# Attention and a mixer on one core: sums of weight quarters on GpSimd over two elements, all queries and keys of the first element loaded ahead, its x transposed within the attention

## The chip, the core and the metric

One core of one Trainium2 chip runs the kernel. Its engines work side by side, each with a queue of instructions of its own that it takes in order: TensorE (PE; the profile shows its weight loads apart, as PEld), VectorE (DVE), ScalarE (ACT), GpSimd (POOL), and SyncE (SP), which issues most DMAs. An instruction that waits for a semaphore holds up all that stand behind it on its engine. The metric is the device time of one execution in microseconds (us).

## The reference

Attention with normalised queries and keys, over 8 batch elements, 12 heads, 448 positions and 64 features a head; its result, laid out as 448 x 768 per element, goes through a mixer: a token layer (448 to 256 to 448, over positions) and a channel layer (768 to 1536 to 768), each added to its input.

```python
q_n, k_n = rmsnorm(q, g_q), rmsnorm(k, g_k)          # over the 64 features of a head
attn = softmax(scale * q_n @ k_n.T) @ v
x = attn.transpose(0, 2, 1, 3).reshape(B, S, H * D)
h = relu(x.transpose(0, 2, 1) @ w_tok1) @ w_tok2
u = x + h.transpose(0, 2, 1)
out = u + relu(u @ w_ch1) @ w_ch2
```

q, k and v are 32-bit floats; the four weight matrices arrive as 64-bit floats and are turned into 32-bit ones by the kernel.

## The kernel before, in words

**The queues are written out by hand.** Work is made as lists of items, each a cost and a function that issues instructions. `merge` (L27) takes lists and deals them into one order, so that each list advances by the same share of its own total cost; an item of cost 0 goes with the one before it. The engines get their instructions in just this order. The main loop (L899 to L925) first merges the attention of element 0 with the first weight conversions. Then for each element b it merges the attention of element b + 1 (`att_items`) with the mixer of element b (`middle_items`, `last_items`), so attention runs one element ahead.

**Attention** goes by pairs of heads, six pairs to an element, 48 in all. `load_qk` (L992) loads a pair's queries and keys with six DMAs on SyncE. `squares` (L1012) squares them on ACT and sums each row on DVE, `roots` (L1038) makes the reciprocal roots on DVE by a chain of ten small instructions, `swap` moves two columns, and `scale` (L285) multiplies the queries by their roots. The keys' roots go into the exponential instead. `trans_qk` (L297) transposes queries and keys on TensorE, and ACT copies them out of PSUM, times the gain. `score` and `score_last` multiply and ACT takes exponentials (L315); `av` and `av_last` multiply by v (L426, L438); the row sums of the exponentials are made on TensorE (L405), after GpSimd (L386) and DVE (L392, L397) have added chunks up (from element 1 on); `denominator` divides on DVE. `att_step(g)` (L484) makes the items of step g; four steps serve two pairs. In steps 0 and 1 of four it prepares the two pairs that follow, and in odd steps it loads a pair. The scales stand on GpSimd, except that of pair 0. Pairs 0 and 1 lie in `hb`, which the mixer needs later for its hidden layer, the others in three tiles that they take in turn. At the start, pair 1 is prepared by `second_pair`, after step 0's items, among which are the squares of pair 2.

Scores, transposes of queries and keys, the row sums `d_ps`, and transposes of x share one PSUM pool of four buffers (tag S); the mixer's products share another of two (tag M).

**The weights.** A chunk of 128 x 512 is loaded (`weight_load`), converted in three steps that are spread over three items, on DVE (L215 to L218), ACT (L226, L228), DVE (L235) and GpSimd (L250), and stored as four quarters to DRAM (`store`): 36 such stages, after four chunks of the token weights. Element 0 uses these quarters plainly (`ch1_first`, `ch2_first`). From element 1 on, the channel layer is done with seven products instead of eight (`ch1`, L726, and `ch2`, L783), for which four sums of quarters are needed besides the quarters themselves. `sum_items` (L180) makes them: item i loads the four quarters of stage i from DRAM, makes a difference of stage i - 1 on DVE (L193), two sums of stage i - 2 in one instruction on GpSimd (L196) and a difference of stage i - 3 on DVE (L200), and stores the four of stage i - 4. That is 40 items: 8 are merged with the second channel layer of element 0, 32 with the first layers of element 1. `load_units` (L642) brings the weights for the products from DRAM, up to five units ahead; where the sums that a unit's group needs are not yet recorded as stored, it loads that unit only when its product is issued.

**The mixer.** `trans_x` transposes x (L575; copies by DVE and ACT in turn, L579 and L581), `tok1` (L596) and `tok2` (L604, added on DVE in L609) are the token layer. In `ch1` the seven results are combined on ACT, DVE and GpSimd (L731 to L765); the fifth product's result is added into r on GpSimd, and DVE needs that r to empty the sixth product's PSUM.

## Time and profile before

| | |
|---|---|
| time, median of 3 runs (lowest to highest) | 1483.64 us (1483.38 to 1483.79) |
| the profiled execution, its span | 1483.56 us, 1481.7 us |
| mean granted clock of TensorE | 0.984 |
| busy in the span: ACT, SyncE's DMAs on q1 | 466.8 us (32%), 48.8% of 16 engines |
| DMA traffic | 219.46 MB, mean 148 GB/s |
| landing of a load of quarters, its store | 3.5 us, 3.6 us (median) |

The profile is one execution on the core. A group of instructions is shown by source line, engine, operation, and tiles as output<-input, with busy time and the mean of one, and with the idle time of its engine just ahead of it and what ended that. Matmuls are pipelined, so a busy TensorE is not one at its peak; the granted clock says at which share of full speed it ran. Rows in order of time give the start, the duration, and in brackets the idle time before and its releaser. The releaser is inferred: where the engine named had long been done, it was something else that the instruction waited for.

### The profile page before, as it was taken

What the parts mean: (1) busy time and instruction counts of PE and PEld (TensorE: products, weight loads), DVE (VectorE), ACT (ScalarE), POOL (GpSimd) and SP (SyncE); (2) the same over time, 40 slices, a digit from 0 to 9 for tenths busy, and PEclk for the clock granted to TensorE, in tenths of its full rate; (3) what the DMA queues carried; (4) which work ended last, traced back from release to release, by engine and by line L of the source; (5) the groups of instructions that cost most, each with busy time, mean ns of one, the idle gap of its engine ahead of it and who ended that gap; (6) DMA issues with size and microseconds to landing.
All of it is one profiled execution on the core that took longest, in us unless ns stands there. A gap on an engine that the chain in (4) does not pass through costs nothing.

```text
span 1481.7 us, 19089 instructions
## 1 busy us (share of the span) xinstructions
PE 1404.9 (95%) x6832; PEld 995.9 (67%) x6832; DVE 711.5 (48%) x1332; ACT 466.8 (32%) x798; POOL 402.1 (27%) x370
## 2 busy tenths in 40 slices
PE   4887889999889999999999999999999999999998
PEld 1333334455568867786777857777677947778997
DVE  5787868616565255533544345432544334331321
ACT  4654444222322234323342233322333223312111
POOL 2222323304453123321333123320332212310320
PEclk9898999999999999999999999999999999999999
DMA  5556766736886524554354625454354624434454
GB/s 138 144 164 194 215 187 189 203 90 193 237 250 183 175 74 139 135 162 113 105 155 127 180 56 156 130 152 129 104 147 126 179 60 129 126 120 133 130 172 122
DMA packets 256810, 219.46 MB, mean 148 GB/s; under 512 B 108004, under 2 KB 215524, under 8 KB 256708
## 3 DMA queue, kind: packets, MB, share of 16 engines
q1 hardware_dynamic: 233506, 206.96, 48.8%
q10 hardware_dynamic: 23074, 11.21, 2.9%
q8 instruction: 56, 0.92, 0.3%
q14 instruction: 46, 0.38, 0.1%
q0 software_dynamic: 128, 0.00, 0.0%
HBM read 188.22 MB, written 29.88 MB: 147 GB/s over the span
## 4 chain that ended last, share of the span: by engine, by line
PE 82%; DVE 8%; DMA 5%; issue 1%; SPq 1%; ACT 1%; POOL 1%; ACTq 0%; DVEq 0%; POOLq 0%
PE m_ps L783 23%; PE m_ps L726 21%; PE s_ps L325 7%; PE o_ps L426 7%; PE m_ps L596 5%; PE m_ps L707 4%; PE m_ps L604 4%; PE t_ps L575 3%; PE m_ps L689 3%; PE t_ps L305 2%; DMA ws<-raw 2%; DMA raw<-ws 2%; PE d_ps L405 2%; PE s_ps L339 1%; PE o_ps L438 1%
## 5 line engine op out<-in xcount | busy, mean ns | idle before, releaser
L783 PE MATMUL m_ps<-hb,unit 128*128 128x224 f32 x1764 | 349.5, 354 | 0.0
L783 PEld LDWEIGHTS m_ps<-hb,unit 128*128 128x128 f32 x1764 | 327.8, 190 | 16.2 <-issue 12.7
L315 ACT ACTIVATE e<-s_ps,rs 128x448 f32<-128x448 f32 x336 | 186.8, 632 | 208.6 <-PE s_ps L325 143.0
L726 PE MATMUL m_ps<-tu,unit 128*128 128x224 f32 x1008 | 204.8, 354 | 2.1 <-DVE hb L731 1.8
L726 PEld LDWEIGHTS m_ps<-tu,unit 128*128 128x128 f32 x1008 | 187.6, 190 | 12.2 <-PE o_ps L426 4.2
L726 PE MATMUL m_ps<-uT,unit 128*128 128x224 f32 x756 | 156.9, 361 | 7.2 <-DVE r L731 3.5
L726 PEld LDWEIGHTS m_ps<-uT,unit 128*128 128x128 f32 x756 | 142.7, 192 | 26.3 <-issue 16.4
L325 PE MATMUL s_ps<-qkT 64*128 64x448 f32 x576 | 141.1, 589 | 2.2 <-ACT qkT L307 1.8
L426 PE MATMUL o_ps<-e,v 128*64 128x448 f32 x576 | 133.3, 566 | 0.0
L295 POOL TENSOR_TENSOR qk<-qk,rs 112x512 f32<-112x512 f32 x46 | 51.5, 1141 | 293.8 <-DVE rs L1063 181.0
L792 POOL TENSOR_TENSOR uT<-uT,r 128x448 f32<-128x448 f32 (+1 forms) x56 | 51.1, 922 | 229.3 <-DVE r L792 147.9
L386 POOL TENSOR_TENSOR es<-e 128x896 f32<-128x896 f32 x42 | 89.7, 2136 | 67.2 <-ACT sq L1025 52.7
L596 PE MATMUL m_ps<-x,w_sb 112*128 112x384 f32 x256 | 92.5, 507 | 8.9 <-DVE x L581 8.9
L307 ACT ACTIVATE qkT<-t_ps,g_t 128x448 f32<-128x448 f32 (+1 forms) x96 | 60.8, 658 | 122.4 <-PE t_ps L305 120.6
L325 PEld LDWEIGHTS s_ps<-qkT 64*128 64x128 f32 x576 | 50.7, 191 | 69.2 <-issue 56.6
L467 DVE STREAM_TRANSPOSE dt<-d_ps 128x448 f32<-128x448 f32 x42 | 27.2, 649 | 142.3 <-PE d_ps L405 142.3
L426 PEld LDWEIGHTS o_ps<-e,v 128*64 128x64 f32 x576 | 33.2, 138 | 86.9 <-issue 83.1
L732 ACT ACTIVATE hb<-hb 128x448 f32<-128x448 f32 x63 | 36.5, 579 | 173.6 <-DVE hb L731 148.2
L792 DVE TENSOR_TENSOR uT<-uT,m_ps 128x448 f32<-128x448 f32 (+1 forms) x70 | 34.0, 502 | 116.5 <-PE m_ps L783 116.4
L392 DVE TENSOR_TENSOR es<-es,e 128x896 f32<-128x896 f32 x42 | 46.6, 1110 | 81.9 <-ACT e L315 64.4
L1029 DVE TENSOR_REDUCE ms<-sq 128x16 f32<-128x1040 f32 (+2 forms) x49 | 59.2, 1207 | 52.5 <-ACT sq L1025 49.4
L731 DVE TENSOR_TENSOR r<-m_ps,r 128x448 f32<-128x448 f32 x63 | 39.2, 621 | 94.2 <-POOL r L731 54.5
(94 smaller groups left out, 1607.6 us busy)
## 6 DMA issues: line engine op xcount, KB each, us to landing
unit<-ws SPq DMA_DIRECT2D x318, 384.0 KB, 3.3
raw<-in_moe_w_ch_dram SPq DMA_DIRECT2D x72, 256.0 KB, 3.4
out_dram<-y ACTq DMA_DIRECT2D x48, 224.0 KB, 3.3
qk<-in_q_dram SPq DMA_DIRECT2D x92, 112.0 KB, 3.5
v<-in_v_dram SPq DMA_DIRECT2D x48, 192.0 KB, 2.7
ws<-stage SPq DMA_DIRECT2D x36, 256.0 KB, 3.7
raw<-ws SPq DMA_DIRECT2D x36, 256.0 KB, 3.5
ws<-raw SPq DMA_DIRECT2D x36, 256.0 KB, 3.6
```

Of the source, the lines that this page charges most:

```text
L307: nc.scalar.mul(to, ps[:, 0:NS * n], g_t[:, i:i + 1])
L315: nc.scalar.activation(out=out, in_=ps[:, 0:S], func=AF.Exp, scale=st["rs", p][:, r:r + 1])
L325: nc.tensor.matmul(out=pss[a][:, 0:S], lhsT=qkT[a * D:(a + 1) * D, o:o + P], rhs=qkT[a * D:(a + 1) * D, 0:S], start=True, stop=True)
L386: nc.gpsimd.tensor_tensor(out=es[:], in0=st["e", p, 0][:], in1=st["e", p, 1][:], op=ALU.add)
L426: nc.tensor.matmul(out=o[a * D:(a + 1) * D, 0:S], lhsT=vt[:, c:c + D], rhs=e[:, a, :], start=start, stop=stop)
L596: nc.tensor.matmul(out=ps[:, 0:HC], lhsT=w1_sb[0:R, c, jc * P:(jc + 1) * P], rhs=st["x", h][0:R, c, :], start=(c == 0), stop=(c == NS - 1))
L604: nc.tensor.matmul(out=ps[:, 0:S], lhsT=st["h1", jc][:, cc * P:(cc + 1) * P], rhs=w2_sb[:, jc].rearrange("p c r -> p (c r)"), start=(jc == ...
L707: nc.tensor.matmul(out=ps[:, 0:S], lhsT=w, rhs=natural(half)[:, :, t, :], start=(half == 0 and t == 0), stop=(half == 1 and t == KF - 1))
L726: nc.tensor.matmul(out=ps[:, j * HS:(j + 1) * HS], lhsT=w[:, t, j, :], rhs=m, start=(t == 0), stop=(t == KC - 1))
L783: nc.tensor.matmul(out=ps[:, j * HS:(j + 1) * HS], lhsT=st["w"](j, t), rhs=hb[:, HB[what], t, :], start=(t == 0), stop=(t == KF - 1))
L792: add = lambda e, o, x, y: e.tensor_tensor(out=o, in0=x, in1=y, op=ALU.add)
L1029: nc.vector.tensor_reduce(out=ms[:, lo:hi], in_=self.sq[0:rows, lo:hi], axis=AX_X, op=ALU.add)
```

## The change

- The sums: all three arithmetic instructions of a stage go to GpSimd, together, two items after the stage's load; the store follows one item later. That makes 39 items, dealt out anew: 6 with the second channel layer of element 0, 6 with the end of element 0, 21 with the first layers of element 1, 6 with its second layer.
- The six pairs of element 0 get places in `hb` and are loaded at the start, between the first five weight chunks. Pair 1 is prepared before the first step; pairs 2 and 3 after step 0, pairs 4 and 5 after step 3, each lot at once. These items now have costs.
- The scales of pairs 1 to 11 go to DVE.
- The first half of x of element 0 (three transposes and their copies) is merged with attention steps 8 to 12, ahead of the token layer; then come the second half's transposes, and the token products after them.
- The squares of queries take only the rows that hold data, so each pair's square is two instructions on ACT, and most of the memsets at the start are replaced by a few.

```diff
@@ -183,27 +183,22 @@
         def one(i):
             n = len(stages)
             if i < n:
-                t = raw_tile()
-                q = st["sum", i] = t[:].rearrange("p n w -> p (n w)").bitcast(F32).rearrange(
-                    "p (q n) -> p q n", q=NQ)
-                st["sum tile", i] = t
-                nc.sync.dma_start(out=q[:, 0:4], in_=slots(i, 0, 4))
-            if 0 <= i - 1 < n:
-                q = st["sum", i - 1]
-                nc.vector.tensor_tensor(out=q[:, 6], in0=q[:, 1], in1=q[:, 0], op=ALU.subtract)
+                t = st["sum", i] = raw_tile()
+                nc.sync.dma_start(out=eight(t)[:, 0:4], in_=slots(i, 0, 4))
             if 0 <= i - 2 < n:
-                q = st["sum", i - 2]
+                q = eight(st["sum", i - 2])
+                nc.gpsimd.tensor_tensor(out=q[:, 6], in0=q[:, 1], in1=q[:, 0], op=ALU.subtract)
                 nc.gpsimd.tensor_tensor(
                     out=q[:, 4:6], in0=q[:, 1:7:5], in1=q[:, 3:4].to_broadcast([P, 2, P]), op=ALU.add)
+                nc.gpsimd.tensor_tensor(out=q[:, 7], in0=q[:, 2], in1=q[:, 5], op=ALU.subtract)
             if 0 <= i - 3 < n:
-                q = st["sum", i - 3]
-                nc.vector.tensor_tensor(out=q[:, 7], in0=q[:, 2], in1=q[:, 5], op=ALU.subtract)
-            if 0 <= i - 4 < n:
-                nc.sync.dma_start(out=slots(i - 4, 4, 8), in_=st.pop(("sum", i - 4))[:, 4:8])
-                st.pop(("sum tile", i - 4))
-                st["summed"] = i - 4 if i - 4 < n - 1 else n
+                nc.sync.dma_start(out=slots(i - 3, 4, 8), in_=eight(st.pop(("sum", i - 3)))[:, 4:8])
+                st["summed"] = i - 3 if i - 3 < n - 1 else n
                 load_units(st["at"])
-        return [(1.0, lambda i=i: one(i)) for i in range(len(stages) + 4)]
+
+        def eight(t):
+            return t[:].rearrange("p n w -> p (n w)").bitcast(F32).rearrange("p (q n) -> p q n", q=NQ)
+        return [(1.0, lambda i=i: one(i)) for i in range(len(stages) + 3)]
 
     def convert_first(i):
 
@@ -553,16 +548,23 @@
             items += [(0.5, lambda pp=pp, part=part: chunk_sums(pp, part)) for pp, part in parts]
         if live and s % 2 == 1 and p + (s + 1) // 2 < NP:
             items.append((0.0, lambda: load_v(p + (s + 1) // 2)))
-        if live and s < 2 and p + 2 + s < NP:
-            items.append((0.0, lambda: pre.squares(p + 2 + s, st)))
-            if s == 1:
-                items.append((0.0, lambda: pre.roots(p + 2, 2, st)))
-                items.append((0.0, lambda: swap(p + 3)))
-                items += [(0.0, lambda i=i: scale(p + 2 + i)) for i in range(2)]
+
+        n = p + 2
+        if g in (0, 3):
+            n = 2 if g == 0 else 4
+            items += [(0.3, lambda i=i: pre.squares(n + i, st)) for i in range(2)]
+        elif live and s < 2 and NPAIR <= n < NP:
+            items.append((0.0, lambda: pre.squares(n + s, st)))
+        if g in (0, 3) or live and s == 1 and NPAIR <= n < NP:
+
+            items.append((0.3 * (n < NPAIR), lambda: pre.roots(n, 2, st)))
+            items.append((0.0, lambda: swap(n + 1)))
+            eng = nc.vector if n < 2 * NPAIR else nc.gpsimd
+            items += [(0.3 * (n < NPAIR), lambda i=i: scale(n + i, eng)) for i in range(2)]
         if turned:
             if not inside:
                 items += [(0.4, lambda i=i: trans_qk(q, i)) for i in range(2)]
-            if q + 3 < NP:
+            if NPAIR <= q + 3 < NP:
                 items.append((0.0, lambda: pre.load_qk(q + 3, st)))
         return items
 
@@ -844,12 +846,13 @@
         items += [(us(6, HS), lambda mp=mp, i=i: ch1(b, mp, i)) for mp in range(KF // 2) for i in range(7)]
         return items, [(us(6, HS), lambda i=i, j=j: ch2(b, 0, i, j)) for i in range(7) for j in range(2)]
 
-    def last_items(b):
+    def last_items(b, sums):
 
 
         single = [(us(6, HS), lambda i=i: ch2(b, 1, i, 0)) for i in range(7)]
         if b == 0:
-            single = [(us(6, S), lambda o=o, h=h: ch2_first(o, h, 2)) for o in range(2) for h in range(2)]
+            single = merge(
+                [(us(6, S), lambda o=o, h=h: ch2_first(o, h, 2)) for o in range(2) for h in range(2)], sums)
         l = turns(b, [0, 1, KC, KC + 1])
         if b + 1 < B:
             l += x_items(b + 1, 0) + x_items(b + 1, 1)
@@ -883,41 +886,38 @@
         trans_qk(0, 0)
     st.pop(("ms", 0))
     load_v(0)
-    weight_load(0)
-    weight_load(1)
-    pre.load_qk(2, st)
-    for i in range(2, 5):
+    for i in range(5):
         weight_load(i)
-    pre.load_qk(3, st)
-
-    def second_pair():
-        pre.squares(1, st)
-        pre.roots(1, 1, st)
-        swap(1)
-        scale(1)
-
+        if 2 + i < NPAIR:
+            pre.load_qk(2 + i, st)
+
+    pre.squares(1, st)
+    pre.roots(1, 1, st)
+    swap(1)
+    scale(1, nc.vector)
     per = NPAIR * 2
     att_items = lambda lo, hi: [it for g in range(lo, hi) for it in att_step(g)]
+
     for _, fn in merge(
-            att_items(0, 1) + [(0.0, second_pair)] + att_items(1, AHEAD * per + 1), weight_items(0, BEFORE)):
+            att_items(0, 8) + merge(att_items(8, AHEAD * per + 1), x_items(0, 0)), weight_items(0, BEFORE)):
         fn()
     left, sums = [], sum_items()
     for b in range(B):
         early, double = middle_items(b)
         if b == 0:
-            begin = [it for h in range(2) for it in x_items(0, h) + tok1_items(0, h)]
+            begin = x_items(0, 1) + tok1_items(0, 0) + tok1_items(0, 1)
             early = merge(begin + early, weight_items(BEFORE, then)) + merge(
-                double, weight_items(then, len(chunks) + 3) + sums[:8])
+                double, weight_items(then, len(chunks) + 3) + sums[:6])
         else:
 
             for _, fn in merge(tok1_items(b, 0), left):
                 fn()
             if b == 1:
-                early = merge(early, sums[8:])
+                early, double = merge(early, sums[12:33]), merge(double, sums[33:])
             early = tok1_items(b, 1) + early + double
         lo = (b + AHEAD) * per + 1
         att = att_items(lo, lo + per) if b + AHEAD < B else []
-        for _, fn in merge(att, early) + last_items(b):
+        for _, fn in merge(att, early) + last_items(b, sums[6:12]):
             fn()
         left = turns(b, [2, KC + 2])
     for _, fn in left:
@@ -941,22 +941,21 @@
 
         n = 2 * self.NS * 2 * D
         flat = self.hb[:].rearrange("p q f s -> p (q f s)")
-        assert flat.shape[-1] >= 2 * n
+        assert flat.shape[-1] >= self.NPAIR * n
         self.st = {}
-        self.qk_t = [const.tile([P, n], F32, name=f"qk_{i}") for i in range(3)]
-        for p in range(2):
-            self.st["qk", p] = flat[:, p * n:(p + 1) * n]
+        qk_t = const.tile([P, 3, n], F32, name="qk_t")
+        self.qk_t = [qk_t[:, i, :] for i in range(3)]
+        hb_t = flat[:, 0:self.NPAIR * n].rearrange("p (i n) -> p i n", n=n)
+        for p in range(self.NPAIR):
+            self.st["qk", p] = hb_t[:, p, :]
         self.v_t = [const.tile([P, (2 * self.NS - 1) * D], F32, name=f"v_{i}") for i in range(2)]
 
         warm = const.tile([P, 1], F32, name="warm")
         nc.vector.memset(warm[:], 1.0)
         nc.scalar.activation(out=warm[:], in_=warm[:], func=AF.Square)
-        self.zeros(nc.vector, self.st["qk", 0])
+        self.zeros(nc.vector, hb_t[:, 0:1])
         self.load_qk(0, self.st, other=nc.scalar)
-        for i, qk in enumerate([self.st["qk", 1]] + self.qk_t):
-            eng = nc.gpsimd if i else nc.vector
-            self.zeros(eng, qk)
-            eng.memset(qk[96:P, 0:n // 2], 0.0)
+        self.zeros(nc.vector, hb_t[:, 1:])
         self.load_qk(1, self.st)
         self.g_t = const.tile([P, 2], F32, name="g_t")
         for i, g in enumerate((g_q, g_k)):
@@ -970,8 +969,11 @@
         self.expo_c = const.tile([P, 1], F32, name="expo_c")
         nc.gpsimd.memset(self.expo_c[:], -896.0 * 2**23)
         self.sq = const.tile([P, 4 * self.NS, D + 1], F32, name="sq")
+
+        nc.gpsimd.memset(self.sq[96:P, 0:2 * self.NS, 0:D], 1.0)
         nc.gpsimd.memset(self.sq[:, 0:4 * self.NS - 2, D:D + 1], D * 1e-6)
         nc.gpsimd.memset(self.sq[:, 4 * self.NS - 2:4 * self.NS, D:D + 1], D * 0.5e-6)
+        self.zeros(nc.gpsimd, qk_t)
         self.st["rs", 0] = const.tile([P, 4 * self.NS], F32, name="rs_0")
         with tc.tile_pool(name="st_0", bufs=1) as self.st_pool:
             self.nt_pool = self.st_pool
@@ -982,8 +984,8 @@
 
         D, P = self.D, 128
         o = qk.shape[-1] - 2 * D
-        eng.memset(qk[D:P, o:o + D], 0.0)
-        eng.memset(qk[0:D, o + D:o + 2 * D], 0.0)
+        eng.memset(qk[D:P, :, o:o + D], 0.0)
+        eng.memset(qk[0:D, :, o + D:o + 2 * D], 0.0)
 
     def heads(self, p):
         b, j = divmod(p, self.NPAIR)
@@ -1022,9 +1024,11 @@
         for lo, hi in halves:
             rows = self.R if hi == 1 else 128
             lo, hi = lo * n, hi * n
-            nc.scalar.activation(
-                out=self.sq[0:rows, lo:hi, 0:D],
-                in_=qk[0:rows, lo * D:hi * D].rearrange("p (r d) -> p r d", d=D), func=AF.Square)
+            for r, at, to in ((self.R, lo, min(hi, n)), (128, max(lo, n), hi)):
+                if at < to:
+                    nc.scalar.activation(
+                        out=self.sq[0:r, at:to, 0:D],
+                        in_=qk[0:r, at * D:to * D].rearrange("p (r d) -> p r d", d=D), func=AF.Square)
             ms = st["ms", p][0:rows, p % 2]
             nc.vector.tensor_reduce(
                 out=ms[:, lo:hi], in_=self.sq[0:rows, lo:hi], axis=AX_X, op=ALU.add)
```

## The prediction

> **What bounds the kernel now.** I read the page first, then the busy time by stage, then the waits of TensorE, then the instructions in order of time around the longest waits. The head of the page:
>
> ```profile
> span 1481.7 us, 19089 instructions
> ...
> PE 1404.9 (95%) x6832; PEld 995.9 (67%) x6832; DVE 711.5 (48%) x1332; ACT 466.8 (32%) x798; POOL 402.1 (27%) x370
> ```
>
> The span is 1481.7 us, the same execution took 1483.56 us, so 1.9 us lie outside; it is within 0.1 us of the median of 1483.64, and I work against 1483.6. TensorE idles only 77 us, so the question is where those are. The busy time by stage (start and end; then busy time and count of PE, weight load, DVE, ACT, POOL; granted clock; DMA share; GB/s), cut at the points where TensorE's order of work changes:
>
> ```profile
> core 0: us, PE busy (x) PEld busy (x) DVE busy (x) ACT busy (x) POOL busy (x), PEclk, DMA share, GB/s
> 0.00:27.30 27.30, 7.06 (x20) 3.34 (x20) 14.70 (x55) 10.58 (x16) 6.57 (x24) 1.00 0.72 177
> 27.30:105.90 78.60, 67.87 (x332) 26.47 (x332) 60.67 (x113) 48.63 (x82) 20.08 (x17) 0.89 0.50 136
> 105.90:222.40 116.50, 96.23 (x326) 43.60 (x324) 89.68 (x138) 49.92 (x86) 33.77 (x26) 0.91 0.68 199
> 222.40:340.00 117.60, 117.40 (x420) 58.59 (x419) 66.66 (x101) 38.51 (x66) 28.30 (x22) 1.00 0.54 153
> 340.00:448.00 108.00, 92.76 (x447) 64.36 (x446) 69.89 (x153) 31.62 (x55) 52.75 (x54) 0.97 0.83 242
> 448.00:1481.70 1033.70, 1023.59 (x5295) 799.58 (x5293) 409.89 (x775) 287.51 (x496) 260.64 (x227) 1.00 0.46 132
> ```
>
> Busy time times clock is the work at full clock. Attention of element 0 (27.3 to 105.9) has 60.4 us of it in 78.6, so 18 are lost; the first layers of element 0 (to 222.4) have 87.6 in 116.5, 29 lost; element 1's first layers (340 to 448) have 90.0 in 108, 18 lost; and 20 go before 27.3. From 222 to 340 and after 448 TensorE is full. So only the early stages and the start of element 1 can pay, some 85 us together, and the change touches just these. There DVE comes next: 77% busy in both early stages. What TensorE waited for, over the span (first two rows of its waits) and then from 340 to 448:
>
> ```profile
> PE t_ps L305 <- POOL hb L295: 10.1, 1, 10.1
> PE t_ps L305 <- POOL stage L250: 9.2, 2, 6.3
> ```
>
> ```profile
> PE m_ps L726 <- DVE hb L731: 4.5, 2, 2.8
> PE m_ps L726 <- DVE r L731: 3.7, 3, 3.0
> PE d_ps L405 <- DVE es L397: 2.9, 2, 2.5
> PE m_ps L604 <- DVE uT L609: 2.5, 2, 1.6
> PE d_ps L405 <- ACT e L315: 1.5, 1, 1.5
> ```
>
> Early it is the preparation of queries and keys; in element 1 nearly every wait names DVE.
>
> **The change, part by part.** *1. The start.* In order of time, with a scale on DVE (first row) for its price:
>
> ```profile
> 9.76 0.69 DVE L295 TENSOR_TENSOR hb<-hb,rs 112x512 f32<-112x512 f32 x1
> ...
> 12.23 4.97 PE L325 MATMUL s_ps<-qkT 64*128 64x448 f32 x12 [0.72 <-ACT qkT L307]
> ...
> 13.08 0.17 DVE L1063 SCALAR_TENSOR_TENSOR rs<-nt,rs 128x8 f32<-128x8 f32 x1
> ...
> 14.24 1.26 SPq L1010 DMA_DIRECT2D qk<-in_k_dram  x2
> ...
> 19.02 1.06 ACT L1025 ACTIVATE sq<-qk 128x1024 f32<-128x1024 f32 x1 [2.24 <-DMA qk<-in_k_dram]
> ...
> 21.38 1.06 ACT L1025 ACTIVATE sq<-hb 128x1024 f32<-128x1024 f32 x1 [1.30 <-DVE ms L1029]
> ...
> 23.50 1.13 ACT L315 ACTIVATE e<-s_ps,rs 128x448 f32<-128x448 f32 x2
> ...
> 26.22 1.04 POOL L295 TENSOR_TENSOR hb<-hb,rs 112x512 f32<-112x512 f32 x1 [19.65 <-DVE rs L1063]
> ...
> 27.32 1.86 PE L305 MATMUL t_ps<-ident,hb 112*128 112x112 f32 x8 [10.12 <-POOL hb L295]
> ...
> 33.61 0.98 PE L339 MATMUL s_ps<-qkT 64*64 64x448 f32 x8
> ...
> 40.26 1.23 ACT L307 ACTIVATE qkT<-t_ps,g_t 128x448 f32<-128x448 f32 x2
> ```
>
> Pair 1's preparation stands behind pair 2's squares, which wait for a load that lands at 19. Its own way from the end of the squares (22.44) to the scale (26.22) is 3.8. Ahead of pair 2, with DVE done with pair 0 at 13.3, pair 1 is scaled on DVE by about 18 (an estimate: 13.3 + 3.8 + 0.69). TensorE's transposes come 9 us sooner. But they do not decide when the next scores start: those need the copies out of PSUM, and ACT's queue now has the squares of pairs 2 and 3 ahead of them. SyncE issues pair 2 until 15.5, then a weight chunk's two DMAs and pair 3's six at 0.63 each, to 20.5; with the same 3.5 from issue to use, pair 3 arrives at 24. Behind it ACT has its squares (1.06, a little more now that they are halved), two passes of a weight chunk (1.4, by the row of L226 in part 2), two exponentials (1.13) and two copies (1.23): 29, against the scores' 33.61 now. That is 4 to 4.5 sooner, less 1.5 to 2 for a TensorE restarting from idle, the price that part 3 finds for such restarts. "At once" is thus an order of issue: pair 5's six, two pairs and two chunks later, are out only near 31. I take -2.5; if the four extra loads slow pair 3, +3; if the squares land early, -6. The memsets that leave GpSimd hide behind the first loads: nothing.
>
> *2. Attention of element 0.* The longest later wait:
>
> ```profile
> 59.71 2.49 POOL L295 TENSOR_TENSOR qk<-qk,rs 112x512 f32<-112x512 f32 x2 [4.68 <-DVE rs L1063]
> ...
> 61.33 2.15 DVE L215 TENSOR_SCALAR e_t<-raw 128x512 uint32<-128x512 uint32 x1
> ...
> 64.83 0.72 ACT L226 ACTIVATE e_t<-e_t,expo_c 128x512 uint32<-128x512 uint32 x1 [5.43 <-DVE e_t L218]
> ...
> 65.37 0.43 DVE L215 TENSOR_SCALAR e_t<-raw 128x512 uint32<-128x512 uint32 x1
> ...
> 66.74 1.83 PE L305 MATMUL t_ps<-ident,qk 112*128 112x112 f32 x8 [6.28 <-POOL stage L250]
> ```
>
> DVE is late with a weight chunk, ACT stands 5.43 before that chunk's pass with the exponentials queued behind it, and TensorE gets no PSUM for its transposes. The change moves eleven scales (pairs 1 to 11) to DVE, 11 x 0.69 = 7.6 us. But the same conversion takes 2.15 beside GpSimd's two scales and 0.43 alone: a pair of scales costs DVE 1.38 there, and gives 1.72 back. I set this to zero; uncovered it is +1.38 for two pairs. The Trainium skill, "SBUF — State Buffer", section "Who interferes with whom", gives this as an exclusive lock on a port that DVE and GpSimd share, the later one blocking fully, also for a DVE instruction with two inputs in SBUF; the trace agrees with 2.15 against 0.43. What remains is order: pairs 4 and 5 are prepared a step or two earlier, in one lump after step 3 (counted from 0), and their loads are long in. The lump (two reductions, roots, scales) still holds DVE for some 8 us, and can hold ACT as above, elsewhere. I take half the 6.28: -3, between -10 (both waits of the 9.2 with their slow restarts) and +4 (the lump stalls step 4 as well). The three transposes of x that come here fill idle TensorE time; each keeps one of four PSUM buffers until its copy, inside the +4.
>
> *3. The first layer's input.* Token mixing waits for copies of the transposed x:
>
> ```profile
> 115.64 7.87 PE L596 MATMUL m_ps<-x,w_sb 112*128 112x384 f32 x16 [5.26 <-DVE x L581]
> ...
> 129.81 4.45 PE L596 MATMUL m_ps<-x,w_sb 112*128 112x384 f32 x8 [3.59 <-DVE x L581]
> ...
> 136.96 2.85 PE L596 MATMUL m_ps<-x,w_sb 112*128 112x384 f32 x8
> ```
>
> Eight at full pace take 2.85; the two runs lost 5.26 + (7.87 - 5.70) = 7.4 and 3.59 + 1.6 = 5.2. The first half of x is now done during attention, so the 7.4 goes. The second half's copies get two products (5.7) as cover, but DVE takes them between conversions, and its conversions are not shortened. I take -7.5, between -12.6 and 0.
>
> *4. The sums.* In element 1, DVE's only wait, its two groups and GpSimd's one, and one moment:
>
> ```profile
> DVE raw L193 <- DMA raw<-ws: 36.1, 18, 4.5
> ```
>
> ```profile
> L193 DVE TENSOR_TENSOR raw<-raw 128x128 f32<-128x128 f32 x29 | 15.2, 523 | 36.3 <-DMA raw<-ws 36.1
> L200 DVE TENSOR_TENSOR raw<-raw 128x128 f32<-128x128 f32 x31 | 12.5, 404 | 0.0
> ```
>
> ```profile
> L196 POOL TENSOR_TENSOR raw<-raw 128x256 f32<-128x256 f32 x30 | 23.4, 785 | 29.4 <-DVE raw L193 25.1 <-PE m_ps L726 3.4 <-POOL es L386 0.3
> ```
>
> ```profile
> 439.29 0.29 DVE L193 TENSOR_TENSOR raw<-raw 128x128 f32<-128x128 f32 x1 [4.31 <-DMA raw<-ws]
> ```
>
> DVE is busy 69.89 and waits 36.1 of 108: it paces the stage, since the subtraction comes one item after its load and the products' adds queue behind it. Afterwards DVE loses the wait and 27.7 of work, and keeps 42. Of the sums 21 fall here, not 31; 12 go where TensorE had no gap. GpSimd takes over: no row shows it at 128x128, so it lies between 0.29 (DVE alone) and 0.785 (GpSimd's twice as wide one); I take 0.45, just above half the latter, since that is the same engine. A stage is then 0.45 + 0.785 + 0.45 = 1.7, and GpSimd has 52.75 - 23.4 + 21 x 1.7 = 65 in a stage of some 97 us, 67%. It computes two items after the load, 9 us at that pitch, beyond the load's wait of 4.5. So of the 18 lost I take 11 back; bounds -16 and 0.
>
> *5. The seam.* The second layer's weights need 30 stages summed; the sums laid into the first layers end at 29, so two units load on demand where the second layer begins. SyncE gets to them only behind a store that waits for GpSimd. No such wait is in the trace; between 0 and the 4.5 of the longest load wait, I take +1.5. The first unit loads of element 1, now fed by sums done before 340, cost nothing. Splitting the squares gives ACT, 32% busy, one instruction more per pair: nothing; on the path it would cost less than an exponential's 0.57 each.
>
> The sum: -2.5 - 3 - 7.5 - 11 + 1.5 = -22.5, so 1461.
>
> **The rivals.** *A. DVE keeps the early pace*: parts 1 to 3 move waits about without removing them. For: the conversions and roots are all still there, and ACT's 5.43 was of this kind. Against: DVE idles 23% of both stages. Only the sums pay: 1483.6 - 11 + 1.5 = 1474.
>
> *B. GpSimd takes DVE's place in element 1*: the adds of L731 and the es sums queue behind 1.7 us blocks, and part 4 yields nothing: 1483.6 - 13 + 1.5 = 1472. For: its share rises from 49% to 67%. Against: its present idle time is a wait for DVE (25.1).
>
> *C. Slower.* In the first layer of element 1, GpSimd's add into r must be done before DVE can empty a PSUM buffer, of which there are two. If each of the 21 blocks falls on that path, the stage loses 21 x 1.7 = 36 instead of 18: +18, and with -13 and +1.5 that is +6.5: 1490. It decides when GpSimd's share comes near the whole, some 95 of 97 us instead of 65, that is, when an op of 128x128 costs 1.2. The Trainium skill, "GPSIMD Engine Reference", section 4.1, speaks for this side: elementwise work belongs on VectorE, about twice as fast. By it the narrow ops would be 0.58 against DVE's 0.29, a stage 1.95 and GpSimd's share 72%; no row here shows one on GpSimd.
>
> *D. All waits named go*, each part at its far end: -6 - 10 - 12.6 - 16 = -45: 1439.
>
> **How the numbers follow.** The forecast, 1461 with its own range of 1450 to 1470, has 0.54; A 0.17, B 0.13, C 0.09, D 0.07. A change of 0.2%, 3 us, is about what a measurement can tell. The forecast, D and most of A and B are faster: 0.86; 0.05 of A and B ends within 0.2%; C is slower: 0.09. The range 1446 to 1478 takes in forecast, A and B, and leaves out C, that 0.05 and about half of D.
>
> **What would show it.** Right: the transposes of pair 1 begin near 18 and step 2's scores near 29; no 5 us wait before the first token mixing; DVE with no wait for raw in element 1, TensorE idle there 3 to 6 us and GpSimd 60 to 70% busy, its 128x128 ops at 0.4 to 0.5 us; a wait of 0 to 4 us for a unit at the second layer. Wrong: TensorE waiting on POOL L731 or es in element 1 for over 10 us (B, C), or ACT waits on DVE of the same total before 222 (A).

## The result, and the profile after

The changed kernel takes 1450.17 us (median of 4 runs, 1447.74 to 1453.44), the kernel before 1483.72 beside it (1483.38 to 1484.2): a ratio of 0.9775, 95% interval 0.9756 to 0.9795, or 33.5 us less. The profiled execution took 1450.25 us with a span of 1448.5, at a mean granted clock of 0.989 (0.984 before). First the head of the page after, then its busy time by stage, with the same columns as in the prediction and cut at the same events: the scores of step 2, the first token product of element 0, and so on to the second channel layer of element 1.

```profile
span 1448.5 us, 19051 instructions
...
PE 1398.2 (97%) x6832; PEld 992.3 (69%) x6832; DVE 681.5 (47%) x1270; ACT 471.5 (33%) x845; POOL 423.3 (29%) x425
```

```profile
core 0: us, PE busy (x) PEld busy (x) DVE busy (x) ACT busy (x) POOL busy (x), PEclk, DMA share, GB/s
0.00:23.90 23.90, 10.59 (x46) 5.20 (x46) 15.86 (x58) 11.38 (x20) 4.18 (x17) 1.00 0.63 158
23.90:107.40 83.50, 71.93 (x345) 28.15 (x345) 64.67 (x126) 50.03 (x90) 15.32 (x13) 0.92 0.58 166
107.40:200.00 92.60, 78.48 (x252) 35.16 (x251) 80.49 (x129) 42.03 (x74) 25.89 (x20) 0.91 0.70 206
200.00:308.60 108.60, 108.60 (x388) 52.31 (x387) 59.12 (x90) 38.62 (x68) 41.38 (x47) 1.00 0.71 207
308.60:413.20 104.60, 103.59 (x506) 70.58 (x505) 51.45 (x92) 37.06 (x67) 65.48 (x85) 1.00 0.69 196
413.20:1448.50 1035.30, 1024.97 (x5304) 800.92 (x5304) 409.89 (x779) 292.39 (x527) 271.04 (x245) 1.00 0.46 135
```

TensorE's idle time fell from 77 to 50 us. In the row from 308.60 to 413.20, which holds element 1 up to its second channel layer, it is busy for 103.59 of 104.60, at full clock. The early rows still show idle time and a clock of 0.91 to 0.92. When the same product starts in the profiled executions of both kernels says where the time went (us from the start of the span; the last column is the whole new set of sums alone in the kernel before, run e1 below):

| TensorE starts | before | after | difference | e1 |
|---|---|---|---|---|
| scores of step 2 | 33.61 | 23.86 | -9.75 | 33.9 |
| first token product, element 0 | 115.64 | 107.37 | -8.3 | 114.0 |
| second token layer, element 0 | 139.65 | 121.65 | -18.0 | 137.65 |
| first channel layer, element 0 | 154.64 | 145.47 | -9.2 | 151.35 |
| second channel layer, element 0 | 248.42 | 235.96 | -12.5 | 243.89 |
| first token product, element 1 | 321.73 | 308.59 | -13.1 | 315.9 |
| second channel layer, element 1 | 447.53 | 413.23 | -34.3 | 420.39 |
| first token product, element 2 | 512.15 | 478.75 | -33.4 | 485.94 |

13.1 us are won before element 1, 20.3 in it, and nothing after it (from element 2's first product to the end both take 970). Single executions differ: the kernels of e2, e4 and e9 below do the early work in the same order as the kernel before and reach element 1 1.4 to 2.8 us sooner, so differences of that size in the table say nothing.

**Element 1.** TensorE's waits between 308.6 and 413.2 (total, times, longest), all there are, and GpSimd's three costliest groups there:

```profile
PE m_ps L728 <- DVE uT L611: 0.8, 1, 0.8
```

```profile
L191 POOL TENSOR_TENSOR raw<-raw 128x256 f32<-128x256 f32 x20 | 15.5, 777 | 1.6
L190 POOL TENSOR_TENSOR raw<-raw 128x128 f32<-128x128 f32 x21 | 12.1, 577 | 0.0
L193 POOL TENSOR_TENSOR raw<-raw 128x128 f32<-128x128 f32 x20 | 10.6, 532 | 1.6
```

The waits of 4.5, 3.7, 2.9 and 2.5 us that named DVE are gone. GpSimd is 63% busy (65.48 of 104.6), and its instructions of 128x128 take 0.53 to 0.58 us.

**The start and the early stages.** In order of time, the first steps:

```profile
18.00 1.02 PE L300 MATMUL t_ps<-ident,hb 112*128 112x112 f32 x8 [1.43 <-ACT sq L1029]
...
21.49 0.63 ACT L1029 ACTIVATE sq<-hb 128x512 f32<-128x512 f32 x1 [0.26 <-DMA hb<-in_k_dram]
...
23.86 0.97 PE L334 MATMUL s_ps<-qkT 64*64 64x448 f32 x4 [1.68 <-ACT e L310]
25.48 1.31 PE L334 MATMUL s_ps<-qkT 64*64 64x448 f32 x4 [0.65 <-ACT qkT L302]
```

Pair 1's transposes begin at 18.00, as forecast, and pair 3's keys have landed by 21.49, where the forecast had 24. The products at 23.86 are pair 0's; those of pair 1, which need its copies out of PSUM, start at 25.48. TensorE's waits over the whole span, the first four:

```profile
PE m_ps L606 <- DVE uT L611: 8.5, 3, 4.6
PE s_ps L334 <- ACT qkT L302: 7.0, 3, 5.7
PE t_ps L300 <- DMA hb<-in_k_dram: 6.2, 1, 6.2
PE s_ps L334 <- ACT e L310: 3.8, 2, 2.1
```

The waits for POOL L295 (10.1) and POOL L250 (9.2) are gone. The 6.2 is the first load of all. New at the top, with 8.5 after 5.5 before, is the second token layer (L606), which waits for its PSUM until DVE has added (L611). In order of time, that wait:

```profile
121.65 3.27 PE L606 MATMUL m_ps<-w_sb,h 128*128 128x448 f32 x8
121.72 1.29 DVE L290 TENSOR_TENSOR qk_t<-qk_t,rs 112x512 f32<-112x512 f32 x2
...
128.87 0.61 DVE L611 TENSOR_TENSOR uT<-uT,m_ps 128x448 f32<-128x448 f32 x1
129.53 3.35 PE L606 MATMUL m_ps<-w_sb,h 128*128 128x448 f32 x4 [4.61 <-DVE uT L611]
```

TensorE reaches the second token layer 18 us earlier, gets two PSUM buffers filled, and then DVE goes through two scales and two conversions before it comes to the add at 128.87. Of the 18 us, 8.8 are given back between there and the first channel layer. The attention of element 0 gives back too: step 2 starts 9.75 sooner, but what follows its last product only 4.3 (101.68 instead of 105.95), with three transposes of x now ahead of it and new waits, such as this one for a PSUM buffer that a transpose of x holds until its copy:

```profile
94.26 1.86 PE L320 MATMUL s_ps<-qkT 64*128 64x448 f32 x2 [2.07 <-DVE x L583]
```

### The profile page after: what moved, and what is told of

Same layout as the page of the kernel before. It is cut to its first block, busy times and chain, and to the rows that moved or that the text cites. A ratio compares the mean times of both kernels' runs of the same rounds, so it can differ in the third digit from the quotient of the medians.

```text
span 1448.5 us, 19051 instructions
## 1 busy us (share of the span) xinstructions
PE 1398.2 (97%) x6832; PEld 992.3 (69%) x6832; DVE 681.5 (47%) x1270; ACT 471.5 (33%) x845; POOL 423.3 (29%) x425
## 4 chain that ended last, share of the span: by engine, by line
PE 88%; DVE 6%; issue 2%; SPq 1%; DMA 1%; ACT 1%; POOL 0%; ACTq 0%; DVEq 0%; POOLq 0%
PE m_ps L728 24%; PE m_ps L785 23%; PE s_ps L320 8%; PE o_ps L421 8%; PE m_ps L598 5%; PE m_ps L606 4%; PE m_ps L709 4%; PE m_ps L691 3%; PE t_ps L577 3%; PE t_ps L300 2%; PE d_ps L400 2%; PE o_ps L433 1%; PE s_ps L334 1%; DVE raw L211 1%; DVE raw L230 1%
## 5 line engine op out<-in xcount | busy, mean ns | idle before, releaser
L728 PE MATMUL m_ps<-uT,unit 128*128 128x224 f32 x756 | 153.8, 356 | 1.8 <-DVE uT L611 1.8
L290 POOL TENSOR_TENSOR qk_t<-qk_t,rs 112x512 f32<-112x512 f32 x36 | 39.3, 1113 | 239.9 <-DVE rs L1067 200.6
L606 PE MATMUL m_ps<-w_sb,h 128*128 128x448 f32 x192 | 80.8, 564 | 8.6 <-DVE uT L611 8.5
L598 PE MATMUL m_ps<-x,w_sb 112*128 112x384 f32 x256 | 88.1, 489 | 0.0
L245 POOL TENSOR_TENSOR stage<-raw 128x512 f32<-128x512 f32 x36 | 41.5, 1154 | 143.5 <-DVE raw L230 66.4
```

What stands on the lines that cost most here:

```text
L598: nc.tensor.matmul(out=ps[:, 0:HC], lhsT=w1_sb[0:R, c, jc * P:(jc + 1) * P], rhs=st["x", h][0:R, c, :], start=(c == 0), stop=(c == NS - 1))
L606: nc.tensor.matmul(out=ps[:, 0:S], lhsT=st["h1", jc][:, cc * P:(cc + 1) * P], rhs=w2_sb[:, jc].rearrange("p c r -> p (c r)"), start=(jc == ...
L728: nc.tensor.matmul(out=ps[:, j * HS:(j + 1) * HS], lhsT=w[:, t, j, :], rhs=m, start=(t == 0), stop=(t == KC - 1))
```

## The experiments

The theory to test was that of the prediction, with a size that was wrong: the sums bring more than forecast because DVE no longer stands behind a load. Its rivals: that it is the dealing of the sums over more stages, the number of buffers, or the engine. For the early part: which of the edits pays, and whether the second token layer's wait can be avoided. Ratios are to runs of the kernel before on the same chip, with 95% intervals.

### e1: all of the new sums, nothing else

The kernel before with the changed `sum_items` and its changed dealing (all lines of the diff that touch `one`, `sums`, `last_items`).

> The kernel before with only the new sums (engines, distance from the load, dealing). In the changed kernel element 1 takes 20 us less from its first token product to element 2's, and the early stages 13 us less. If the sums alone make the former: 1463 to 1465, with TensorE idle for 1 to 3 us in element 1's first layers. Rival: the early stages' gain also eases element 1, and the sums alone give about the 9.5 us of the forecast: 1474.

Measured: 1457.81 us, ratio 0.9833 [0.9816, 0.9849], that is 25 us less, against 9.5 in the sum of the prediction's parts 4 and 5, and below the 1463 to 1465 expected: part of the gain comes before element 1. Element 1, from its first token product to element 2's, takes 170.0 us (190.4 before, 170.2 in the full change). TensorE's waits between 300 and 520:

```profile
PE m_ps L721 <- DVE uT L604: 0.8, 1, 0.8
```

So three quarters of the gain is the sums, and the early parts add only 7.6 in medians.

### e2, e3: the two halves of it

e2 takes the new `one(i)` (three instructions on GpSimd two items after the load, the store at i - 3) and deals as before, 8 items and then the other 31. e3 takes the new dealing only:

```diff
-                double, weight_items(then, len(chunks) + 3) + sums[:8])
+                double, weight_items(then, len(chunks) + 3) + sums[:6])
...
-                early = merge(early, sums[8:])
+                early, double = merge(early, sums[12:33]), merge(double, sums[33:])
...
-        for _, fn in merge(att, early) + last_items(b):
+        for _, fn in merge(att, early) + last_items(b, sums[6:12]):
```

> The kernel before with the sums' arithmetic on GpSimd two items after the load, dealt as before (8 items with element 0's second layer, 31 with element 1's first layers). If DVE's wait for loads was what paced element 1, most of the 20 us goes without the spreading: 1465 to 1469. If GpSimd, at 31 x 1.9 us in that stage, takes DVE's place: 1475 to 1484. If it is the spreading that pays: 1480 or more.

> The kernel before with the sums dealt as in the change (6, 6, 21, the rest) but on the old engines and at the old distances. If DVE's wait for loads paces, 21 of 31 waits stay in the first layers, longer pitch makes each a little shorter, and the rest moves to the second layer: a gain of 6 to 10, 1474 to 1478. If the number of sums and their DMA traffic in that stage was the bound: a gain of 15 or more, 1468 or less.

Measured: e2 1473.78, ratio 0.9933 [0.9916, 0.9949], 9.0 less; e3 1467.5, ratio 0.989 [0.9873, 0.9906], 15.3 less. The two add up to 24.3 of e1's 25, and the dealing, which the prediction had no price for, is the larger. e2 fell between its two expectations; e3 came out where the rival had put it, by which the number of sums in that stage, or their DMA traffic, is the bound. In e3 DVE still makes its differences and still waits for loads (first fence: a row of DVE's waits over the span), and the wait for a unit at the second channel layer that the prediction had expected at the seam appears (second fence: TensorE's waits):

```profile
DVE raw L193 <- DMA raw<-ws: 22.2, 8, 6.7
```

```profile
PE m_ps L783 <- DMA unit<-ws: 2.5, 5, 1.0
```

Between the two channel layers of element 1 (348.0 to 425.8) TensorE no longer idles in e3, with the sums still on DVE:

```profile
348.00:425.80 77.80, 77.78 (x404) 58.65 (x404) 48.24 (x96) 27.43 (x47) 34.67 (x36) 0.98 0.77 216
```

In e2 GpSimd has all 31 items in the stage, and is the busiest it gets in any run (from element 1's first token product to its second channel layer):

```profile
319.70:433.80 114.10, 108.24 (x513) 73.77 (x511) 52.83 (x92) 36.94 (x64) 78.25 (x110) 0.97 0.72 207
```

78.25 of 114.1 is 69%; that stage takes 114.1 us against 125.8 before and 104.6 in the full change. For the whole of it both were needed, fewer items in the stage and the new order.

### e4: only the distance from the load

If DVE waits because the first difference comes one item after its load, one item more must help.

```diff
-            if 0 <= i - 1 < n:
-                q = st["sum", i - 1]
+            if 0 <= i - 2 < n:
+                q = st["sum", i - 2]
                 nc.vector.tensor_tensor(out=q[:, 6], in0=q[:, 1], in1=q[:, 0], op=ALU.subtract)
```

> The kernel before with the first difference on DVE two items after its load instead of one, nothing else. If it is DVE's wait for the load, not its work, then its 36 us fall to under 10 and 12 to 17 us are gained: 1467 to 1472. If DVE's 28 us of sums count as much, DVE goes from 106 of 108 us taken to some 75, which is still under the whole, so this rival has to show in waits of TensorE on DVE that stay: 1476 or more.

Measured: 1481.66, ratio 0.9993 [0.9983, 1.0004]: nothing that can be told from no change. DVE's wait in the span is shorter but there:

```profile
DVE raw L193 <- DMA raw<-ws: 26.8, 12, 4.6
```

DVE's wait was to fall to under 10 and 12 to 17 us were to be gained; so the reason given in part 4 falls. Something holds up the loads themselves.

### e9: one more buffer

What does is seen on SyncE. Its waits in the kernel before, between the first and the second channel layer of element 1 (355.9 to 447.5), first row, and then its issues in order of time:

```profile
SPq L190 <- DMA ws<-raw: 24.6, 20, 2.8
```

```profile
433.66 0.38 SPq L202 DMA_DIRECT2D ws<-raw  x1
435.26 0.36 SPq L190 DMA_DIRECT2D raw<-ws  x1
...
437.77 0.36 SPq L190 DMA_DIRECT2D raw<-ws  x1
438.23 1.94 SPq L202 DMA_DIRECT2D ws<-raw  x2
```

There are five buffers for the stages. The load of stage i (L190) needs the buffer of stage i - 5, and with the store at i - 4 this stage is stored (L202) just one item earlier: the load at 437.77 waits for the store issued at 433.66, 4.1 us before it (a store lands after 3.6 in the median), and DVE's next difference, on what that load brought, starts 4.1 later, at 441.85. So items can hardly follow each other faster than a store lands: the 24 loads of that stretch come 3.54 us apart on average (356.38 to 437.77). With six buffers the store comes two items ahead of the load that needs it:

```diff
-    raw_pool = pool("raw_pool", 5)
+    raw_pool = pool("raw_pool", 6)
...
-    y_pool = pool("y_pool", 3)
+    y_pool = pool("y_pool", 2)
```

(The outputs give up a buffer to make room.)

> The kernel before with six buffers instead of five for the tiles of the sums and weight chunks (two instead of three for the output tiles makes the room). Theory: five buffers pace element 1. A load there waits until the store of the stage five back has landed, so store and load, 3.6 and 3.5 us, stand one behind the other in each round; a later use, as in the run before, cannot help. Then one buffer more takes most of DVE's 36 us of waits away and gains 8 to 12: 1471 to 1475. Rival: the DMA traffic of that stage, 83% of the engines' time, is the bound: no gain, 1480 to 1484.

Measured: 1473.18, ratio 0.9944 [0.9927, 0.9961], 9.7 less. DVE's wait over the span falls from 36.1 to 19.4, and the loads' wait on the stores' landing in the same stage (353.1 to 433.7) from 24.6 to 14.1; the 23 loads there come 3.25 apart. The weight chunks use these buffers too, but the gain is in element 1: 180.9 from its first token product to element 2's, for 190.4 before.

```profile
DVE raw L193 <- DMA raw<-ws: 19.4, 10, 3.6
```

```profile
SPq L190 <- DMA ws<-raw: 14.1, 12, 2.8
```

The bytes are the same, so this gain doesn't come from less traffic. With the round loosened the DMA engines are busier, 0.95 of that stretch for 0.86 before (355.9 to 447.5):

```profile
353.10:433.70 80.60, 76.44 (x391) 59.47 (x390) 56.77 (x114) 26.24 (x45) 44.16 (x43) 0.96 0.95 272
```

Element 1 is still 10.7 us longer there than in the change (170.2), so traffic may be the next limit. The new dealing takes both rounds and bytes out of the stage (0.77 in e3), and which of the two its 15 us come from no run separates. As for the other two runs, the same row of SyncE's waits is not shorter than before in e4, which gains nothing, and shorter in e2, which gains as much as e9:

```profile
SPq L190 <- DMA ws<-raw: 26.8, 16, 2.8
```

```profile
SPq L187 <- DMA ws<-raw: 16.7, 13, 2.4
```

(e4 first, then e2.) That row is a hint and no measure of a gain: in e3 it is 26.4 and in the change 20.6, with 16 and 19 loads between the same two layers instead of 24, and TensorE does not come to wait for them. In e2 the store stands at i - 3, one item sooner, which leaves the same two items between store and load as a sixth buffer does. The sixth buffer is shown. That the earlier store is what e2 gains from was not tried alone; e10 only says, for the new dealing, that it is not the engine.

### e10: the changed kernel with its sums on DVE

```diff
-                nc.gpsimd.tensor_tensor(out=q[:, 6], in0=q[:, 1], in1=q[:, 0], op=ALU.subtract)
-                nc.gpsimd.tensor_tensor(
+                nc.vector.tensor_tensor(out=q[:, 6], in0=q[:, 1], in1=q[:, 0], op=ALU.subtract)
+                nc.vector.tensor_tensor(
...
-                nc.gpsimd.tensor_tensor(out=q[:, 7], in0=q[:, 2], in1=q[:, 5], op=ALU.subtract)
+                nc.vector.tensor_tensor(out=q[:, 7], in0=q[:, 2], in1=q[:, 5], op=ALU.subtract)
```

> The changed kernel with the three instructions of a stage on DVE instead of GpSimd, at the same place and with the same dealing. If the buffers' round and the dealing pay, and the engine does not matter: within 3 us of the changed kernel, 1448 to 1453. If DVE's work in element 1 matters, as the forecast had it (28 us off DVE): DVE gets 21 stages of 1.2 us or more there and waits for loads ahead of the products' adds: 1457 to 1465.

Measured: 1452.76, ratio 0.9801 [0.9785, 0.9817], 2.6 us above the change in medians, with intervals that overlap. Element 1's stage (308 to 413):

```profile
308.00:413.00 105.00, 100.48 (x493) 69.50 (x492) 72.01 (x153) 35.90 (x65) 27.79 (x24) 1.00 0.70 201
```

```profile
PE m_ps L728 <- DVE uT L611: 2.5, 1, 2.5
PE m_ps L606 <- DVE uT L611: 2.1, 1, 2.1
```

DVE has 72.01 of 105 (51.45 of 104.6 in the change), more than the 69.89 of 108 with which it "paces the stage" in the prediction, and TensorE waits for it for only a few us. The engine that makes the sums is worth little under this dealing, 2.6 us in medians; the order and the dealing bring the rest.

### e6: only pair 1 prepared first

The kernel before, with the lines of `second_pair` moved ahead of the merge and its scale on DVE; no further loads are moved.

```diff
-    def second_pair():
-        pre.squares(1, st)
...
-        scale(1)
-
+    pre.squares(1, st)
+    pre.roots(1, 1, st)
+    swap(1)
+    scale(1, nc.vector)
...
-            att_items(0, 1) + [(0.0, second_pair)] + att_items(1, AHEAD * per + 1), weight_items(0, BEFORE)):
+            att_items(0, AHEAD * per + 1), weight_items(0, BEFORE)):
```

> The kernel before with only pair 1 prepared ahead of step 0 and its scale on DVE; loads and later preparations as before. If the order of pair 1 is what made the start 9.8 us earlier: step 2 of attention begins near 26 instead of 33.6. Of that, DVE's pace in the attention should take back half or more: 1478 to 1481. Rival: it is the earlier loads, and step 2 begins after 30: 1482 to 1484.

Measured: 1476.45, ratio 0.9959 [0.9945, 0.9973], 6.5 less, more than the 2 to 5 expected. In order of time:

```profile
18.34 1.06 ACT L1023 ACTIVATE sq<-qk 128x1024 f32<-128x1024 f32 x1 [1.48 <-DMA qk<-in_k_dram]
...
22.04 1.87 PE L339 MATMUL s_ps<-qkT 64*64 64x448 f32 x8
...
25.31 1.06 ACT L1023 ACTIVATE sq<-qk 128x1024 f32<-128x1024 f32 x1 [2.42 <-DMA qk<-in_k_dram]
```

Step 2's scores start at 22.04, sooner than in the change (23.86), since pair 3's load and squares come after them. So the early start is pair 1's place alone; the loads of all six pairs ahead aren't needed for it. Later this kernel still has the old waits, as its two longest groups show:

```profile
PE t_ps L305 <- POOL stage L250: 9.3, 2, 6.3
PE m_ps L596 <- DVE x L581: 8.8, 2, 5.3
```

### e7, e8: one edit taken back out of the change

e7 puts the transposes of x back behind the attention, each half ahead of its products:

```diff
-            att_items(0, 8) + merge(att_items(8, AHEAD * per + 1), x_items(0, 0)), weight_items(0, BEFORE)):
+            att_items(0, AHEAD * per + 1), weight_items(0, BEFORE)):
...
-            begin = x_items(0, 1) + tok1_items(0, 0) + tok1_items(0, 1)
+            begin = [it for h in range(2) for it in x_items(0, h) + tok1_items(0, h)]
```

> The changed kernel with x of element 0 transposed after the attention, as before. If the move pays as in the forecast, the wait ahead of the first token product returns: 4 to 8 us more, 1454 to 1458. Rival: what the move wins is given back at the next wait for DVE, that of the second token layer (6 us in the changed kernel), so the time stays within 2 us: 1448 to 1452.

Measured: 1456.61, ratio 0.9826 [0.9807, 0.9845], 6.4 above the change, and the old wait is back (TensorE's longest):

```profile
PE m_ps L598 <- DVE x L583: 10.3, 2, 5.4
```

The second token layer starts at 134.53 there (121.65 in the change), 12.9 later, but the first channel layer at 148.22, only 2.7 later than 145.47. Most of what x wins is lost at that layer, in the profile. Element 1 starts 4.7 later (313.29 for 308.59), and the rest of the 6.4 comes within element 1 (173.3 us for 170.2), away from the wait that the move was meant for.

e8 puts the scales of pairs 2 to 11 back on GpSimd (`eng = nc.gpsimd`).

> The changed kernel with the scales of pairs 2 to 11 back on GpSimd (pair 1's stays on DVE). The forecast held the move for neutral, since a pair of scales on GpSimd blocks DVE for 1.7 us and costs it 1.4 on its own: within 2 us of the changed kernel, 1448 to 1452. If DVE's own work is what binds the early stages: 1444 to 1447. If GpSimd's lateness ahead of the transposes is the cost: 1453 or more.

Measured: 1453.98, ratio 0.981 [0.9796, 0.9823], 3.8 above the change; the intervals only just don't touch, so it is probably slower, by an amount that is open. The profiled execution was its fastest, at 1450.93, and so tells little of where. One wait for GpSimd's last step of a weight chunk is back, of 2.7 us (TensorE's transposes in L300, for L245).

### e11, e12, e13: against the wait at the second token layer

e11 gives the token layer's items of element 0 half their cost, so that fewer conversions are dealt in among them:

```diff
+            begin, early = [[(c * (0.5 if i < n else 1.0), fn) for i, (c, fn) in enumerate(l)] for l, n in ((begin, 99), (early, 6))]
```

e12 prepares pairs 2 to 5 in the old steps, one pair's squares a step and at cost 0, instead of both pairs of a lot after steps 0 and 3; the loads stay ahead. e13 is both.

```diff
-        if g in (0, 3):
-            n = 2 if g == 0 else 4
-            items += [(0.3, lambda i=i: pre.squares(n + i, st)) for i in range(2)]
-        elif live and s < 2 and NPAIR <= n < NP:
+        if live and s < 2 and n < NP:
             items.append((0.0, lambda: pre.squares(n + s, st)))
-        if g in (0, 3) or live and s == 1 and NPAIR <= n < NP:
+        if live and s == 1 and n < NP:
```

> The changed kernel with the token layer's items of element 0 dealt at half their cost, so that some two weight chunks (2.9 us of DVE each) fewer come among them and more later. If DVE's conversions are what the second token layer waits for (6 us and a slow restart): 3 to 6 us less, 1444 to 1447. If the conversions moved later only make a later wait there, at the weights of the first channel layer: 1449 to 1453.

> The changed kernel with pairs 2 to 5 prepared at the steps of before (0, 1 and 4, 5) and at cost 0, all loads still ahead. Counted one by one, sums (25), pair 1 first (6.5) and x (6.4) give 38 of the 33.5 measured, so the two lots after steps 0 and 3 may cost some 4 us. If so: 1445 to 1447. If the parts overlap and the lots are neutral: 1449 to 1452. If the lots are what lets x go into the attention: 1454 or more.

> The changed kernel with both of the last two edits: token items dealt at half cost, and pairs 2 to 5 prepared at the steps of before. If the two gains (2.1 and 3.7 in the medians) stand apart: 1443 to 1445. If each frees DVE for the same wait of the second token layer: 1446 to 1448. It also tells whether the slowest run of the latter kernel, with a 3.9 us wait for a load of v, was an accident.

| | median us | ratio | lowest to highest |
|---|---|---|---|
| the change | 1450.17 | 0.9775 [0.9756, 0.9795] | 1447.74 to 1453.44 |
| e11 | 1448.1 | 0.9764 [0.975, 0.9777] | 1446.26 to 1449.03 |
| e12 | 1446.44 | 0.9756 [0.9742, 0.9769] | 1445.66 to 1451.55 |
| e13 | 1446.36 | 0.9753 [0.9739, 0.9768] | 1445.28 to 1447.11 |

All three medians lie below the change's, and all three intervals overlap with its own: that any of them beats the change isn't shown. e11 fell between its two expectations; in its profiled execution element 1 starts at 305.88, 2.7 sooner than in the change. e12 lies where it was expected if the lots cost some 4 us, and e13, which adds nothing to e12 in medians, where it was if both edits ease the same wait; neither is shown by that. Two of TensorE's waits in e13:

```profile
PE m_ps L602 <- DVE uT L607: 6.2, 2, 3.7
...
PE o_ps L433 <- DMA v<-in_v_dram: 3.8, 1, 3.8
```

The second token layer's wait (L602 there) is smaller (8.5 in the change), not gone, and a wait for v of 3.8 is new; e12 has one of 3.9 in its profiled execution, its slowest. Since e13 has it in its fastest, it is not what made that one slow. Both kernels issue v behind the loads of queries and keys, as the change does. Earlier attention meets v's load; that v lands late because of those loads was not tried.

## Why the prediction was right

**Faster, inside the range, 11 us below the number.** 1461 had been forecast, 1450.2 came, 4 us from the fast end of the range. The sum was -2.5 - 3 - 7.5 - 11 + 1.5; the experiments give it other sizes: 25 for the 9.5 of the sums, 7.6 for the 13 of the early parts. That the two errors partly cancel is luck: with the sums at 25 and the early parts at their 13 it would have been 1445.6, just outside the range.

**Part 4 with part 5 is the step that failed**: "since the subtraction comes one item after its load", so that 11 of 18 us come back and 1.5 are paid at the seam. Alone the sums bring 25 (e1). DVE, which "paces the stage" in the prediction, doesn't: with 72 us of work on DVE in that stage TensorE idles 4.5 us (e10). The distance brings nothing (e4); loads stood behind the landing of a store one item ahead, a round that the step did not count, and one more buffer brings 9.7 (e9). The dealing brings 15 (e3), where the prediction only counted 21 items for 31 as a reason for GpSimd's share. It put the lost time in element 1 at 18 as read between 340 and 448; in fact 20.3 were won from its first token product on, and the stage ended with 1.0 us idle, at full clock. At the seam there is no wait: TensorE's only one in the stage is 0.8. GpSimd's load was foreseen (65.5 us for 65), its small instructions less so: 0.53 to 0.58 for 0.45. By the Trainium skill, "GPSIMD Engine Reference", section 4.1, about twice DVE's time, the estimate was 0.58, and 0.53 to 0.58 against DVE's 0.29 agrees with it. Its advice to leave such work to VectorE gains nothing here: with the sums on DVE the time is 2.6 us longer in medians (e10).

**Part 1 was too small at its own place**: -9.75 at step 2's scores for -2.5. Its mechanism holds, as e6 shows (pair 1 first, -6.5 in all); the step that failed is "pair 3 arrives at 24". It was taken from an issue-to-use time of 3.5 and had landed by 21.49: the weight chunk ahead of it is one DMA and not the two counted, so the last of its six loads goes out at 18.86, and lands 2.5 later. The products that need pair 1's copies start at 25.48 for 29. The caution that the extra loads may cost was not needed at the start.

**Part 2 had the wrong sign in the attention**, +5.5 in place of -3: ACT's and DVE's waits moved, as rival A has it for this part. With part 1 it makes -4.3 by the end of attention, for a forecast of -5.5. The trade by which "a pair of scales costs DVE 1.38 there, and gives 1.72 back", set to zero, may be worth up to some 4 (e8, barely clear of noise).

**Part 3 was near in size**: 7.5 forecast, 6.4 by e7, of which 4.7 show before element 1. The prediction did not see that the next layer's add would queue behind DVE's scales and conversions; that is why -18.0 at the second token layer becomes -9.2 behind it.

**The early parts together**: forecast -13. The -13.1 of the table looks like it, but part of that belongs to the sums: e1 reaches element 1 5.8 us ahead of the kernel before, and e3, which has only the dealing, 5.1 (316.59), more than the 2.8 by which executions differ. Element 1's attention is dealt there against a list with two sums fewer. Between e1 and the change it is -7.3 in the profiled executions and -7.6 in medians. The three edits measured singly (6.5, 6.4, 3.8) would make 16.7, so they don't add. Where the rest of the 16.7 goes is only partly seen (the second token layer's 8.5); e11 to e13 left it unsettled.

**The rivals.** A's sign, ACT's waits on DVE before 222, could not tell: they were 47.3 us before and are 50.6 after. The early parts brought about half of their 13, so A was partly right. B fell: with all 31 items in the stage and GpSimd at 69% (e2), the sums still gained 9 us. C needed an op of 128x128 at 1.2; it measured half that. D, 1439, is as near to the result as the forecast. Of its parts the one on the sums came true, with 25 for 16 and nearly all waits in element 1 gone; the early ones, 28.6 together, did not.

## What to carry to other kernels

When a consumer waits for a load, look at what the load waited for: in a ring of buffers that are stored and reloaded, count the items between the store and the load that takes its place, and compare them with the store's landing time. An item more between load and use does nothing then; a buffer more does (a store one item earlier should, but was not tried alone). Background work that is dealt into one stage is best judged by what that stage can carry: a third of it moved to stages where TensorE had no gap brought more than the choice of engine. In the change it cost about 1 us there (65.5 from element 1's second channel layer to element 2, for 64.6 before), in e3, where units came late, 4.8.

## What the runs showed of the hardware

DVE's conversion step L211 in the change takes 1.34 us on average at 128x512, and 0.69 in the two early ones of 112x512, which come with no GpSimd instruction beside them:

```profile
L211 DVE SCALAR_TENSOR_TENSOR raw<-raw,e_t 128x512 f32<-128x512 uint32 x36 | 48.3, 1341 | 3.0
...
L211 DVE SCALAR_TENSOR_TENSOR raw<-raw,e_t 112x512 f32<-112x512 uint32 x2 | 1.4, 694 | 0.1
```

In order of time, once DVE is first by 0.02 us, and once GpSimd (the last step of the chunk before) by 0.34:

```profile
111.90 0.69 DVE L211 SCALAR_TENSOR_TENSOR raw<-raw,e_t 128x512 f32<-128x512 uint32 x1
111.92 1.57 POOL L245 TENSOR_TENSOR stage<-raw 128x512 f32<-128x512 f32 x1 [3.41 <-DVE e_t L210]
114.60 1.14 POOL L245 TENSOR_TENSOR stage<-raw 128x512 f32<-128x512 f32 x1 [1.10 <-ACT e_t L221]
114.94 1.35 DVE L211 SCALAR_TENSOR_TENSOR raw<-raw,e_t 128x512 f32<-128x512 uint32 x1
```

In these two, whichever starts first takes its usual time, and the other is longer by most of what the first has left: DVE's 0.69 becomes 1.35, GpSimd's 1.14 becomes 1.57. This agrees with the Trainium skill, "SBUF — State Buffer", section "Who interferes with whom", by which a DVE instruction with two inputs in SBUF contends with a GpSimd one that reads SBUF, and the order of issue decides which of them blocks. Of the 36, all but one take 1.2 us or more: 35 x 0.65 = 23 us of DVE up to 247, and up to 200 it is about as busy as TensorE. That GpSimd is the reason each time was seen only in the rows shown. No run took this overlap away, so what it is worth in time is open.
